# A smaller descriptor area for GpSimd's DMAs, and three more weight slabs kept in SBUF

## Chip, cores and metric

The kernel runs on one core of a Trainium2 chip. The metric is the device time of one execution in microseconds, from the first to the last instruction of the core. Three runs of the kernel before gave 2266.03 us (median), 2262.88 us (lowest) and 2273.69 us (highest). The profile is of one execution of 2273.2 us.

## The reference

The input `x` has 2048 rows of 1024 (bfloat16). It is layer-normed to `xn`, and the output is `x + A(xn) + B(xn)`.

- `B` is a dense block: `gelu(xn @ w1 + b1) @ w2 + b2`, with 3584 hidden columns.
- `A` is a recurrent attention layer. The 2048 rows are cut into 64 segments of 32 rows. Each segment puts 8 memory rows before its 32 rows, and runs 32-head attention (heads of 128) on the 40 rows:

```
for s in range(64):
    h = concat([mem, xn[32*s : 32*s+32]])          # 40 rows of 1024
    q, k, v = h @ Wq, h @ Wk, h @ Wv               # 1024 -> 4096 each
    p = softmax(mask(q @ k.T * scale))
    o = (p @ v) @ Wo                               # 4096 -> 1024
    mem, out[s] = o[:8], o[8:]
```

The new memory is part of the output of the segment before, so the 64 segments can't be computed together: every one needs all of Wq, Wk, Wv and Wo again. These are 4 x 1024 x 4096 bfloat16 numbers, 33.6 MB, which is more than SBUF holds.

## The kernel before

**Two stages.** The first stage (to about 360 us) is the dense block. It works on groups of 512 rows (`tg` from 0 to 3): transposed rows times w1 (L391), the gelu on ScalarE and VectorE (L384 to L407), times w2 (L438, and L471 in the last group). Its sum with `x` goes to HBM as the rows `R_n`, and the transposed normed rows go to `hr_d`, from which the second stage loads them segment by segment. The second stage is the loop over 64 segments (L567).

**Weights in units.** The four weights are cut into 64 units of [128, 2048] bfloat16: 4 KB in each partition, 512 KB in all. `pass_order` (L49) gives the order in which every segment uses them: eight units each of K, Q, V for the first 16 heads, eight each of K, Q, V for the other 16, then 16 units of O. A unit of K, Q or V is used by four matmuls of 512 columns that write four column groups of the array (L598), a unit of O by eight matmuls of 256 columns (L746).

43 of the units are resident: they are loaded once and stay in SBUF for all 64 segments. The other 21 are streamed: every segment loads them anew. The string `PLACED` (L65) says for each position of the order whether it is streamed. Streamed units are first copied in HBM to a dense layout (`copies`, L162, fetched at L425 in the first group of the dense block).

**The stream.** There are six stream buffers (`STREAM_BUFS`, L46). `start_stream` (L185) is called once for each streamed unit that has been used (`unit_done`, L542): the buffer of the unit that has just been used is given to the unit six further on in the stream, and SyncE issues its 512 KB DMA (L193). One streamed unit of each segment, `IN_PSUM` (L70, the fourth), doesn't come by DMA after the first segment: the first segment leaves it in two banks of PSUM (`keep_unit`, L518), and ScalarE and VectorE copy it from there to the buffer (L190, L191). So 20 DMAs of 512 KB are made per segment.

**Rows of several segments together.** Of each segment, 24 rows and the 8 memory rows go through the matmuls at once (`hT`); the other 8 rows of four segments are gathered and go through them once in four segments (`hL`). So one segment in four (`i4`, the segment's number modulo 4) has its K units used twice, another its Q units, another its V units, and another has the O units used with twice as many rows.

**Where SBUF goes.** The dense block's slabs (`PLACES`, L156: xn, w1, w2, gT) are 41 places of 4 KB per partition. The first six become the stream buffers, the other 35 take resident units as the dense block lets go of them (`fetch_resident`, L175, called at L458, L479 and L480). Eight more resident units are loaded in the first segment (`fetch_late`, L535). 16 KB of each partition, at address 0, are set aside by the library for the descriptors of the DMAs that GpSimd issues ("DynamicDMAScratchLoc").

**GpSimd's DMAs.** In the second stage GpSimd issues the small DMAs: the next segment's rows (`load_x_rows`, L199 to L202, called at L818 after the last V unit), the rows to be added to (L801, L807), the results (L852, L877 to L885), and in the first segments the rows `R_n` of the last group (L352). All of them are issued in the program's order on one queue. Some wait in the list `small` and are issued one or two at a time by `unit_done` after a streamed unit.

**The end of a segment.** After the 16 O units, ScalarE takes the sum from PSUM (L840), TensorE transposes the new memory rows (L222), VectorE puts them beside the rows that L201 loaded (L223), and the next segment's K pass starts.

Of the kernel before, what the change touches and what calls it, by code (L numbers as in the profile page):

```python
# [10 lines left out]
BF16 = mybir.dt.bfloat16  # L11
# [5 lines left out]
P = 128  # L17
S = 2048
# [23 lines left out]


NUNIT = 64
STREAMED = 21
STREAM_BUFS = 6  # L46


# [13 lines left out]


ORDER = pass_order()
PLACED = "S..S...S" "...S..S." "..S..S.." "S...S..S" "..S..S.S" "..S..S.." "S..S..S." ".S..S..S"  # L65
IS_STREAMED = {unit: PLACED[n] == "S" for n, unit in enumerate(ORDER)}
assert PLACED.count("S") == STREAMED
RESIDENT = [unit for unit in ORDER if not IS_STREAMED[unit]]
# [6 lines left out]
def kernel(  # L75
# [16 lines left out]
    nc = tc.nc  # L92
# [20 lines left out]
    outL_d = dram.tile([NGRP, 2 * SEG, DM], BF16, name="outL_d")  # L113
    outM_d = dram.tile([NGRP, P, 256], BF16, name="outM_d")

    slabs = ctx.enter_context(tc.tile_pool(name="slabs", bufs=1))
    consts = ctx.enter_context(tc.tile_pool(name="consts", bufs=1))
    hrp = ctx.enter_context(tc.tile_pool(name="hrp", bufs=1))
    ctx.enter_context(tc.manual_schedule())

    def slab(place):
        return slabs.tile([P, 2048], BF16, name="u", tag=place)


# [30 lines left out]

    PLACES = [f"xn{k}" for k in range(4)] + [f"w1_{k}" for k in range(16)]  # L156
    PLACES += [f"w2_{k}" for k in range(14)] + [f"gT{k}" for k in range(7)]
    STREAM_PLACES, RES_PLACES = PLACES[:STREAM_BUFS], PLACES[STREAM_BUFS:]
    res_tiles = {}


# [5 lines left out]
    def fetch(t, unit):  # L167
        w, i, u = unit
        if w == "O":
            h = 4 * i + 2 * u  # L170
            nc.sync.dma_start(out=t.rearrange("p (h d) -> p h d", d=DM), in_=Wo_v[:, h:h + 2, :])
        else:
            nc.sync.dma_start(out=t, in_=W_v[w][:, i, 2048 * u:2048 * u + 2048])

    def fetch_resident(n0, n1):  # L175
        for place, unit in list(zip(RES_PLACES, RESIDENT))[n0:n1]:
            res_tiles[unit] = slab(place)[:, :]
            fetch(res_tiles[unit], unit)
# [51 lines left out]
    with tc.tile_pool(name="ma", bufs=2) as ma, tc.tile_pool(name="mps", bufs=6, space=PSUM) as mps:  # L230
# [143 lines left out]
        for tg in range(4):  # L374
            last = tg == 3
            if last:

                load_x_rows(0)
                load_left_rows(0)
            gts = [slab(f"gT{i}")[:, :].rearrange("p (c t) -> p c t", c=4) for i in range(7)]  # L380

            def gelu_tail(fb, u, xb):
                sg = ma.tile([P, 512], BF16, name="g_sg")
                nc.scalar.activation(out=sg[:, :], in_=u[:, :], func=ACT.Sigmoid, scale=GELU_C)  # L384
                nc.vector.tensor_tensor(out=gts[fb // 4][:, fb % 4, :], in0=sg[:, :], in1=xb[:, :], op=ALU.mult)

            pend = None
            for fb in range(FC):
                ps = mps.tile([P, 512], F32, name="ps")
                for kt in range(KT):  # L390
                    nc.tensor.matmul(  # L391
                        ps[:, :].rearrange("p (s t) -> p s t", t=SEG),
                        lhsT=w1_sb[fb // 14 * 8 + kt][:, (fb % 14) * P:(fb % 14 + 1) * P],
                        rhs=xnT[kt // 4][:, :, kt % 4, :],
                        start=(kt == 0),
                        stop=(kt == KT - 1),
                    )
                xb = ma.tile([P, 512], BF16, name="g_xb", bufs=3)
                nc.scalar.activation(  # L399
                    out=xb[:, :], in_=ps[:, :], func=ACT.Identity, bias=b1col[:, fb:fb + 1], scale=1.0  # L400
                )
                u = ma.tile([P, 512], BF16, name="g_u")
                nc.vector.tensor_tensor(out=u[:, :], in0=xb[:, :], in1=xb[:, :], op=ALU.mult)
                nc.vector.tensor_scalar(
                    out=u[:, :], in0=u[:, :], scalar1=0.044715, scalar2=1.0, op0=ALU.mult, op1=ALU.add
                )
                nc.vector.tensor_tensor(out=u[:, :], in0=u[:, :], in1=xb[:, :], op=ALU.mult)  # L407
                if pend is not None:
                    gelu_tail(*pend)
                pend = (fb, u, xb)  # L410
            gelu_tail(*pend)

            if tg == 0:
                for nb in range(2):
                    cs = slice(nb * 512, nb * 512 + 512)
                    ps = mps.tile([P, 512], F32, name="ps")
                    nc.tensor.matmul(ps[:, :], lhsT=ones[0:1, :], rhs=b2row[0:1, cs], start=True, stop=True)
                    nc.scalar.copy(out=b2bc[:, cs], in_=ps[:, :])

            if not last:  # L420
                xnT = new_xnT(tg + 1)
                for t in range(4):
                    xtoks[4 * tg + 4 + t] = load_x(4 * tg + 4 + t)
                if tg == 0:
                    for unit, c in copies.items():  # L425
                        fetch(c, unit)
                for t in range(4):
                    ln_stats(4 * tg + 4 + t, xtoks[4 * tg + 4 + t])
                ln_rstd(4 * tg + 4, 4 * tg + 8)
                for t in range(4):  # L430
                    ttg = 4 * tg + t
                    xn = ln_apply(ttg + 4)
                    rsb = xtoks[ttg]
                    for nb in range(2):
                        cs = slice(nb * 512, (nb + 1) * 512)
                        ps = mps.tile([P, 512], F32, name="ps")
                        for fc in range(FC):
                            nc.tensor.matmul(  # L438
                                ps[:, :],
                                lhsT=gts[fc // 4][:, fc % 4, t * P:(t + 1) * P],  # L440
                                rhs=w2_sb[fc // 2][:, fc % 2, cs],
                                start=(fc == 0),
                                stop=(fc == FC - 1),
                            )
                        nc.vector.tensor_tensor(out=ps[:, :], in0=ps[:, :], in1=b2bc[:, cs], op=ALU.add)
                        nc.vector.tensor_tensor(out=rsb[:, cs], in0=ps[:, :], in1=rsb[:, cs], op=ALU.add)
                        if nb == 1:
                            turn_x(ttg + 4, xn, xnT)
                    keep_R(ttg, rsb)
                keep_xT(tg + 1, xnT)  # L450
                for t in range(4):
                    turn_R(4 * tg + t)
            else:


                for _ in range(STREAM_BUFS):
                    start_stream()
                fetch_resident(0, 16)  # L458
                put_mem(o_sb, nxt["hT"], mps.tile([P, KT, P], BF16, name="pT", bufs=2))
                pss = [mps.tile([P, 512], F32, name="ps") for _ in range(6)]  # L460
                pss += [mps.tile([P, 512], F32, name="pT", bufs=2) for _ in range(2)]
                for n in range(8):
                    cs = slice((n % 2) * 512, (n % 2 + 1) * 512)
                    nc.tensor.matmul(pss[n][:, :], lhsT=ones[0:1, :], rhs=b2row[0:1, cs], start=True, stop=False)
                    nc.tensor.matmul(
                        pss[n][:, :], lhsT=ident[:, :], rhs=xtoks[4 * tg + n // 2][:, cs], start=False, stop=False
                    )
                for fc in range(FC):
                    for t in range(4):
                        for nb in range(2):  # L470
                            nc.tensor.matmul(  # L471
                                pss[2 * t + nb][:, :],
                                lhsT=gts[fc // 4][:, fc % 4, t * P:(t + 1) * P],
                                rhs=w2_sb[fc // 2][:, fc % 2, nb * 512:nb * 512 + 512],
                                start=False,
                                stop=(fc == FC - 1),
                            )
                    if fc % 2:
                        fetch_resident(16 + fc // 2, 17 + fc // 2)  # L479
                fetch_resident(30, 37)  # L480
                for n in range(8):
                    cs = slice((n % 2) * 512, (n % 2 + 1) * 512)
                    cp = nc.scalar.copy if n % 2 else nc.vector.tensor_copy
                    cp(out=xtoks[4 * tg + n // 2][:, cs], in_=pss[n][:, :])
                for t in range(4):
                    keep_R(4 * tg + t, xtoks[4 * tg + t])
# [436 lines left out]
```

The softmax here doesn't subtract the row's maximum and nothing guards it: scores larger than these inputs give would overflow.

## Time and profile before

| what | before |
|---|---|
| median of three runs | 2266.03 us |
| span of the profile | 2273.2 us |
| TensorE busy | 2028.4 us (89%) |
| VectorE, ScalarE, GpSimd busy | 828.8, 660.5, 269.6 us |
| moved by DMA | 761.91 MB, 335 GB/s over the span |
| of it by the queue of SyncE | 736.71 MB |
| of it by GpSimd's DMAs | 16.87 MB in 16,000 packets |
| DMAs of 512 KB from the copies (L193) | 1281 |

The page's slices are 57 us each. "Busy" of TensorE includes matmuls whose ends are modelled, so that a busy TensorE isn't one at its peak, and a matmul that waits for less than its modelled end shows no idle time. A row of the chain of waits that reads "DMA u<-Wc_K" is the transfer of a streamed unit of K into a stream buffer. "issue" is time for which the profile shows no cause. A line such as L598 is line 598 of the kernel.

### The profile page before, as it was taken

What the parts mean: (1) busy time and instruction counts of PE and PEld (TensorE: products, weight loads), DVE (VectorE), ACT (ScalarE), POOL (GpSimd) and SP (SyncE); (2) the same over time, 40 slices, a digit from 0 to 9 for tenths busy, and PEclk for the clock granted to TensorE, in tenths of its full rate; (3) what the DMA queues carried; (4) which work ended last, traced back from release to release, by engine and by line L of the source; (5) the groups of instructions that cost most, each with busy time, mean ns of one, the idle gap of its engine ahead of it and who ended that gap; (6) DMA issues with size and microseconds to landing.
All of it is one profiled execution on the core that took longest, in us unless ns stands there. A gap on an engine that the chain in (4) does not pass through costs nothing.

```text
span 2273.2 us, 79002 instructions
## 1 busy us (share of the span) xinstructions
PE 2028.4 (89%) x34707; PEld 1047.3 (46%) x34707; DVE 828.8 (36%) x2264; ACT 660.5 (29%) x1540; POOL 269.6 (12%) x527
## 2 busy tenths in 40 slices
PE   7999999888898988898989898989898889888986
PEld 3444444344444444444544444444444444444443
DVE  6574844133333333333333333333323333333332
ACT  5251623122222222222222222222222222222222
POOL 0000000024111011111111111010111111111110
PEclk9999999999999999999999999999999999999999
DMA  9621116899999999999999999999999999999997
GB/s 323 205 71 33 51 51 230 296 395 391 388 402 371 384 373 388 362 382 386 386 379 401 377 397 374 395 372 374 376 372 372 376 383 400 378 379 378 401 382 276
DMA packets 256629, 761.91 MB, mean 335 GB/s; under 512 B 50923, under 2 KB 68283, under 8 KB 256284
## 3 DMA queue, kind: packets, MB, share of 16 engines
q1 hardware_dynamic: 234748, 736.71, 85.3%
q0 software_dynamic: 16000, 16.87, 2.2%
q8 instruction: 271, 4.44, 0.8%
q10 hardware_dynamic: 5536, 3.30, 0.5%
q14 instruction: 74, 0.61, 0.1%
HBM read 742.52 MB, written 33.10 MB: 341 GB/s over the span
## 4 chain that ended last, share of the span: by engine, by line
PE 66%; DMA 24%; DVE 3%; issue 3%; ACT 3%; POOL 0%; ACTq 0%; POOLq 0%; DVEq 0%; SPq 0%
PE acc L598 30%; PE acc L746 9%; PE ps L391 9%; DMA u<-Wc_O 7%; DMA u<-Wc_K 7%; PE ps L438 6%; DMA u<-Wc_V 5%; DMA u<-Wc_Q 4%; PE mixed L555 4%; PE acc L722 2%; PE ps L471 2%; PE mixed L685 1%; DVE d_oL L632 1%; PE mixed L681 1%; ACT d_oL L840 1%
## 5 line engine op out<-in xcount | busy, mean ns | idle before, releaser
L598 PE MATMUL acc<-u,hr 128*32 128x512 bf16 x12288 | 939.8, 391 | 74.6 <-DMA u<-Wc_Q 23.6
L598 PEld LDWEIGHTS <-hr 128*32 128x32 bf16 x12288 | 315.6, 97 | 379.0 <-issue 136.8
L598 PE MATMUL acc<-u,hrL 128*32 128x512 bf16 x3072 | 304.0, 384 | 3.5 <-issue 2.4
L626 ACT CAST d_oL<-acc 128x512 bf16<-128x512 f32 x192 | 112.4, 585 | 479.5 <-PE acc L598 435.4
L391 PE MATMUL ps<-u 128*128 128x512 bf16 x896 | 196.0, 382 | 2.6 <-ACT u L297 2.6
L642 DVE COPY kT<-mixed 128x512 bf16<-128x512 bf16 x128 | 54.4, 425 | 370.0 <-PE mixed L555 370.0
L746 PEld LDWEIGHTS <-b_oL 128*32 128x32 bf16 (+1 forms) x3552 | 136.1, 115 | 74.5 <-issue 64.0
L746 PE MATMUL acc<-W_O,b_oL 128*32 128x256 bf16 (+1 forms) x2220 | 130.0, 298 | 24.9 <-issue 24.9
L438 PE MATMUL ps<-u 128*128 128x512 bf16 x672 | 147.0, 379 | 0.0
L696 ACT ACTIVATE pr<-mixed 128x224 bf16<-128x224 f32 x128 | 45.7, 357 | 332.6 <-PE mixed L691 316.5
L391 PEld LDWEIGHTS <-u 128*128 128x128 bf16 x896 | 88.1, 98 | 109.2 <-issue 4.9
L746 PE MATMUL acc<-u,d_oL 128*32 128x256 bf16 (+1 forms) x2220 | 130.8, 294 | 4.9 <-DMA u<-Wc_O 2.5
L746 PEld LDWEIGHTS <-d_oL 128*32 128x32 bf16 (+1 forms) x3552 | 118.2, 112 | 33.1 <-issue 10.6
L652 DVE COPY b_oL<-mixed 128x512 bf16<-128x512 bf16 x128 | 54.4, 425 | 207.2 <-PE mixed L555 207.2
L746 PE MATMUL acc<-u,b_oL 128*32 128x256 bf16 (+1 forms) x1332 | 94.0, 300 | 26.1 <-DMA u<-Wc_O 15.2
L555 PEld LDWEIGHTS <-d_oL 128*128 128x128 bf16 x1020 | 59.4, 98 | 124.5 <-ACT d_oL L626 54.8
L598 PEld LDWEIGHTS <-hrL 128*32 128x32 bf16 x3072 | 86.0, 97 | 66.0 <-issue 9.0
L201 POOL DMA_DIRECT2D hr<-hr_d x63 | 34.6, 548 | 611.6 <-PE acc L598 351.3
L555 PE MATMUL mixed<-ident,d_oL 128*128 128x128 bf16 x896 | 89.3, 222 | 13.1 <-DVE d_oL L632 8.6
L438 PEld LDWEIGHTS <-u 128*128 128x128 bf16 x672 | 65.3, 98 | 77.4 <-DVE g_u L407 0.4
L734 ACT CAST d_oL<-acc 128x128 bf16<-128x128 f32 x128 | 50.9, 397 | 171.7 <-PE acc L728 171.7
L399 ACT ACTIVATE g_xb<-ps,b1col 128x512 bf16<-128x512 f32 x112 | 76.9, 686 | 61.0 <-PE ps L391 59.9
(126 smaller groups left out, 2408.4 us busy)
## 6 DMA issues: line engine op xcount, KB each, us to landing
u<-Wc_K SPq DMA_DIRECT2D x384, 512.0 KB
u<-Wc_O SPq DMA_DIRECT2D x384, 512.0 KB
u<-Wc_Q SPq DMA_DIRECT2D x257, 512.0 KB
u<-Wc_V SPq DMA_DIRECT2D x256, 512.0 KB
u<-in_B_w_dram SPq DMA_DIRECT2D x16, 448.0 KB
u<-in_B_w_dram SPq DMA_DIRECT2D x14, 512.0 KB
u<-in_A_Wv_dram SPq DMA_DIRECT2D x12, 512.0 KB
u<-in_A_Wq_dram SPq DMA_DIRECT2D x11, 512.0 KB
```

Source lines behind the costliest of these rows:

```text
L391: nc.tensor.matmul(ps[:, :].rearrange("p (s t) -> p s t", t=SEG), lhsT=w1_sb[fb // 14 * 8 + kt][:, (fb % 14) * P:(fb % 14 + 1) * P], rhs=x ...
L399: nc.scalar.activation(out=xb[:, :], in_=ps[:, :], func=ACT.Identity, bias=b1col[:, fb:fb + 1], scale=1.0)
L438: nc.tensor.matmul(ps[:, :], lhsT=gts[fc // 4][:, fc % 4, t * P:(t + 1) * P], rhs=w2_sb[fc // 2][:, fc % 2, cs], start=(fc == 0), stop=(fc ...
L471: nc.tensor.matmul(pss[2 * t + nb][:, :], lhsT=gts[fc // 4][:, fc % 4, t * P:(t + 1) * P], rhs=w2_sb[fc // 2][:, fc % 2, nb * 512:nb * 512 ...
L555: nc.tensor.transpose(dst[:, c, :], nat[:, c * P:(c + 1) * P], ident[:, :])
L598: nc.tensor.matmul(acc[32 * j:32 * j + 32, :], lhsT=lhs[:, i, :], rhs=t[:, 512 * j:512 * j + 512], start=(i == seq[0]), stop=(i == seq[-1] ...
L626: nc.scalar.copy(out=nat[:, :], in_=ps[:, :])
L642: nc.vector.tensor_copy(out=st["kT"][:, :, :], in_=by_head(tr))
L652: nc.vector.tensor_copy(out=st["qT"][:, :, 0:32], in_=by_head(tr))
L696: nc.scalar.activation(out=pr[:, :], in_=mixed[:, 0:224], func=ACT.Exp, scale=INV_SQRT_DH)
L734: cp(out=(o_both if left_o else o_main)[u][:, hs, 0:32], in_=oV[b][:, :, 0:32])
L746: nc.tensor.matmul(acc[r:r + n // 8, 0:n], lhsT=lhs[:, 4 * (i % 4) + 2 * u + k, :], rhs=t[:, 1024 * k + n * jq:1024 * k + n * jq + n], sta ...
```

## The change

The area for GpSimd's descriptors becomes 4 KB of each partition instead of 16 KB. The 12 KB that this frees hold three more resident units (`low0` to `low2`, tensors at fixed addresses right behind the smaller area). So 46 units are resident and 18 streamed, and one of the 18 stays in PSUM as before: 17 DMAs of 512 KB per segment instead of 20. The string `PLACED` is written anew, with the 18 streamed positions spread over the order: 2, 2, 2, 2, 2 and 3 in the passes K, Q, V, K, Q, V, and 2 and 3 in the two halves of O.

The three new places come first among the resident places. They are free from the start, so their units are fetched in the first group of the dense block, behind the copies, on SyncE's queue. The other calls of `fetch_resident` are shifted by three, so that each place of the dense block still takes its unit at the same point.

```diff
-STREAMED = 21
+STREAMED = 18
+LOW = 3
+SCRATCH = 4096
 STREAM_BUFS = 6
...
-PLACED = "S..S...S" "...S..S." "..S..S.." "S...S..S" "..S..S.S" "..S..S.." "S..S..S." ".S..S..S"
+PLACED = "S....S.." ".S....S." "..S..S.." ".S...S.." ".S..S..." "S..S...S" "..S...S." ".S...S.S"
...
+    place = nc.lookup_mloc("DynamicDMAScratchLoc")
+    assert place.addr == 0 and list(place.dims) == [P, SCRATCH + LOW * 4096]
+    nc.dynamic_dma_scratch_size = SCRATCH
+    place.dims = [P, SCRATCH]
+    nc.lookup_mls("DynamicDMAScratchLoc").tensor_shape = [P, SCRATCH]
+    low = {
+        f"low{k}": nc.alloc_sbuf_tensor_at(f"low{k}", [P, 2048], BF16, offset=SCRATCH + 4096 * k) for k in range(LOW)
+    }
...
     def slab(place):
+        if place in low:
+            return low[place]
         return slabs.tile([P, 2048], BF16, name="u", tag=place)
...
-    STREAM_PLACES, RES_PLACES = PLACES[:STREAM_BUFS], PLACES[STREAM_BUFS:]
+    STREAM_PLACES, RES_PLACES = PLACES[:STREAM_BUFS], list(low) + PLACES[STREAM_BUFS:]
...
                     for unit, c in copies.items():
                         fetch(c, unit)
+                    fetch_resident(0, LOW)
...
-                fetch_resident(0, 16)
+                fetch_resident(LOW, LOW + 16)
...
-                        fetch_resident(16 + fc // 2, 17 + fc // 2)
-                fetch_resident(30, 37)
+                        fetch_resident(LOW + 16 + fc // 2, LOW + 17 + fc // 2)
+                fetch_resident(LOW + 30, LOW + 37)
```

## The prediction

> **What bounds the kernel now.** I first cut the span into its stages with busy times by stretch, then asked the DMA view of the long stage what moves, and then the waits of TensorE in it. The ends of the stages are the two ends of VectorE's copies at L223, which close a segment: 64 of them, the first at 372 us, the second at 472.2, the last at 2231.0.
>
> ```profile
> 0.00:372.50 372.50, 354.49 (x1711) 163.70 (x1711) 235.98 (x593) 158.55 (x257) 11.54 (x43) 1.00 0.38 120
> 372.50:472.40 99.90, 87.75 (x947) 41.78 (x946) 16.84 (x41) 10.84 (x25) 0.70 (x1) 0.98 0.91 342
> 472.40:2231.00 1758.60, 1561.46 (x31640) 827.96 (x31640) 566.83 (x1608) 483.55 (x1240) 253.49 (x476) 0.98 1.00 383
> 2231.00:2273.20 42.20, 24.69 (x410) 13.86 (x410) 9.12 (x24) 7.58 (x18) 3.86 (x7) 0.88 0.59 230
> ```
>
> Columns: stretch, length, busy time of TensorE, its weight loads, VectorE, ScalarE and GpSimd, granted clock, DMA share, GB/s. The third row is what counts: 62 segments in 1758.6 us, 28.36 us each, with the 16 DMA engines busy all the time (1.00) at 383 GB/s. TensorE is idle for 1758.6 - 1561.5 = 197 us of it.
>
> ```profile
> DMA packets 199274, 673.43 MB, mean 383 GB/s; under 512 B 29294, under 2 KB 36258, under 8 KB 198966
> q1 hardware_dynamic: 178546, 650.13, 95.8%
> q0 software_dynamic: 15712, 16.60, 2.8%
> q8 instruction: 247, 4.05, 0.9%
> ```
>
> This is the same stretch by queue. The stream is 96% of it: 62 x 20 x 0.524 MB = 650 MB. Everything else is 23 MB. So the kernel is bound by its stream of weights.
>
> ```profile
> PE acc L746 <- issue: 38.9, 30, 2.5
> PE mixed L222 <- ACT d_oL L840: 28.7, 61, 0.5
> PE acc L598 <- DMA u<-Wc_Q: 20.4, 38, 1.6
> PE acc L598 <- DMA u<-Wc_K: 18.2, 45, 1.4
> PE acc L746 <- DMA u<-Wc_O: 17.4, 36, 1.0
> ...
> PE acc L598 <- DMA u<-Wc_V: 7.8, 18, 1.5
> ```
>
> TensorE's waits in it (us in total, times, longest). Those for streamed units sum to 20.4 + 18.2 + 17.4 + 7.8 = 63.8 us in 137 waits. That is smaller than a DMA-bound kernel suggests, because a wait hides behind the modelled end of the matmul before it:
>
> ```profile
> 1216.46 0.39 PE L598 MATMUL acc<-u,hr 128*32 128x512 bf16 x4
> 1216.68 0.39 PE L598 MATMUL acc<-u,hrL 128*32 128x512 bf16 x4
> 1216.89 0.39 PE L598 MATMUL acc<-u,hr 128*32 128x512 bf16 x4
> ```
>
> Start, length, and four matmuls each: they follow each other by 0.215 us and are drawn 0.39 long, so every visible wait cost 0.175 us more than shown, and shorter ones aren't seen. 137 x 0.175 = 24 us. The DMA waits are then 63.8 + 24 = 88 us, or 1.42 us per segment.
>
> **What the Trainium skill says.** "DMA: Bandwidth & Descriptors", Terms: a descriptor is 16 B, and those of GpSimd's DMAs are written to rings in SBUF; that area is what shrinks. No row shows a ring. "DMA: Bandwidth & Descriptors", Specifications: about 358 GB/s from HBM per core; the trace has 383, and I use that. "Runtime: NRT & Kernel Launch", Instruction fetch mechanics: instructions come in 16 KB blocks of 256, mostly hidden. The trace has the blocks (4.05 MB in 247 packets), but not always the hiding: the 38.9 us of L746 above have no cause but "issue", and L598 and L722 to L728 add 5.3. "TensorE: Matmul & The Clock Gate", What's actually happening: after an idle window of about 3.4 us the clock is halved. The trace agrees in kind: from 925.3 to 932.1 us the granted clock is 0.50, right after an issue wait of 2.44 us.
>
> **The change part by part.**
>
> *Three fewer transfers per segment.* 673.4 - 62 x 3 x 0.524 = 575.9 MB are left; at 383 GB/s that is 1504 us, 24.25 us per segment. The engines stop being the bound if TensorE needs longer than that, and it does: taking the DMA waits from the segment leaves 28.36 - 1.42 = 26.94 us. At that pace the engines would be 90% busy, with six buffers to run ahead by (six transfers of 1.37 us, 8 us of cover), so I expect DMA waits to be nearly gone, not only reduced. Even spacing is what allows that: the gaps of the new string are 2 to 5 positions within a segment.
>
> *What goes with these waits.* The mean granted clock is 0.98 in the stretch; the missing 0.02 x 1758.6 = 35 us are 0.57 us per segment lost at half clock. The halvings follow long waits, some for DMAs and some for instructions, so I take half of it away: 0.28. DMA waits below 0.175 us, which no view shows, I bound by 0 and 0.3 and take 0.15. Sum: 26.94 - 0.28 - 0.15 = 26.5 us. What stays is the instruction waits (38.9 + 5.3 = 44 us, 0.7 per segment), the end of a segment (L840, L222, L223), and the matmuls. The saving is 28.36 - 26.5 = 1.86 us, times 62: 115 us.
>
> *The first segment* (second row) is mostly bound by its loads: 34 MB in 99.9 us. It needs three fewer units, since those were fetched in the dense block: 3 x 0.524 MB at 383 GB/s is 4 us. The last segment with the output (42 us) has its DMA engines at 0.59, and its O pass is of the double kind: I count nothing.
>
> *The three early fetches, and 18 copies instead of 21.* They lie in the first group of the dense block, behind 354 of 372 us of busy TensorE and with the DMA engines at 0.38. Nothing.
>
> *PSUM unit, small DMAs.* The kept unit is the fourth streamed one still, and its buffer comes free at the same place of the order as before, the second O unit of the second half (number 57): ScalarE's 1.01 us and VectorE's 0.69 us stay where they are. The list `small` is emptied at 18 places instead of 21, for five entries or fewer in most segments. Nothing.
>
> *The 4 KB area.* GpSimd has 15,712 packets in 62 segments on 16 engines, 16 per engine and segment. If a packet is about one descriptor of 16 B, and 4 KB hold 256 of them for an engine, the area takes 16 segments' worth, while a DMA lands in about 5 us. The estimate rests on the skill's 16 B. I take no cost. The upper bound is a GpSimd that must wait for its DMA before to land. Queued behind it would be the next segment's rows, for which TensorE waits:
>
> ```profile
> DMA to landing us min/median/max: 4.7/5.4/6.6
> ```
>
> That is the landing time of L201's transfers; next is one of them in GpSimd's timeline, then VectorE's copy that needs its tile:
>
> ```profile
> 1230.90 0.53 POOL L201 DMA_DIRECT2D hr<-hr_d  x1 [0.96 <-PE acc L598]
> ```
>
> ```profile
> 1237.40 0.19 DVE L223 COPY hr<-mixed 128x64 bf16<-128x64 bf16 x1 [0.84 <-PE mixed L222]
> ```
>
> The rows are asked for at 1230.90 and needed at 1237.40: 6.5 us for a landing of 5.4 (6.6 at most). It fits, with 1.1 us to spare, and the O pass there is not much stretched by DMA waits, so a faster kernel keeps about that.
>
> Sum: 2266 - 115 - 4 = 2147 us.
>
> **The rivals.**
>
> *TensorE alone is left (chance 0.15).* All half clock and most instruction waits were the crowded DMA engines' doing. 28.36 - 1.42 - 0.57 - 0.7 - 0.15 = 25.5 us: 2266 - 62 x 2.84 - 4 = 2086. For it: the instruction blocks travel on the same engines. Against: the waits gather at L746, where instructions are used fastest (16 matmuls and weight loads per 0.217 us), which the change doesn't touch.
>
> *The stream still sets the pace (0.2).* Transfers start only when a buffer comes free, and with gaps the engines may not hold 383 GB/s. At the 342 GB/s of the first segment 9.29 MB take 27.2 us: 2266 - 62 x 1.16 - 4 = 2190. Against: these 342 come from a stretch with a share of 0.91.
>
> *The small area costs what the stream saves (0.07).* If GpSimd waited for one landing (5.4 us) ahead of the rows' load in each segment, 5.4 - 1.1 = 4.3 us would stand at every segment's end: 26.5 + 4.3 = 30.8, and 2266 + 62 x 2.44 - 4 = 2413 us, slower than before. If it met this only in the segments with O's double rows (one in four), 1.1 us on average, the time would be 2215. Against: the 16 segments of room. I give 0.04 to the slow end and 0.03 to between.
>
> **How the numbers follow.** The forecast (26.5 +- 0.4 us per segment) has 0.58. Its unknowns are the invisible waits (0 to 0.3) and the clock (0 to 0.57 of it): 25.9 to 27.0 us, or 2110 to 2178 us. The range reaches to both neighbours, to all of the second rival's 2190 and nearly to the first's 2086: 2090 to 2192. Faster 0.93; within 0.5% 0.03; slower 0.04.
>
> **What would show it.** The DMA share of the long stretch falls from 1.00 to about 0.9, its bytes to 576 MB; TensorE's waits for `u<-Wc_` fall from 63.8 to below 15 us; "issue" at L746 stays near 39 us; segments take 26.5 us; the stretch of the first segment falls by 4 us; GpSimd's busy time and the landing at L201 stay. A landing that ends the wait of L598 or L223, or GpSimd waiting in front of its DMAs, would show the small area's cost. The prediction is wrong if the DMA share stays at 1.00.

## The result, and the profile after

The changed kernel takes 2156.18 us (median; 2152.33 to 2160.28) against 2269.86 us of the kernel before in the same comparison. The ratio is 0.9486, with a 95% interval of 0.9451 to 0.9522: 114 us, or 5%, faster. 2147 us were forecast.

In the changed kernel the lines have moved: the matmuls of K, Q and V are L613 (before L598), those of O L761 (L746), the stream's DMAs L207 (L193), the rows' load L215 (L201), the copy that closes a segment L237 (L223).

Busy times by stretch, with the same columns as before (stretch, length, busy time of TensorE, weight loads, VectorE, ScalarE, GpSimd, granted clock, DMA share, GB/s). The stretches are again cut at the copy L237:

```profile
0.00:371.40 371.40, 353.61 (x1711) 163.47 (x1711) 236.05 (x593) 158.57 (x257) 11.54 (x43) 1.00 0.38 120
371.40:467.30 95.90, 87.44 (x947) 42.06 (x946) 16.81 (x41) 10.67 (x25) 0.70 (x1) 0.98 0.89 340
467.30:2118.50 1651.20, 1513.67 (x31640) 817.68 (x31640) 567.13 (x1608) 483.24 (x1240) 253.55 (x476) 0.99 0.96 349
2118.50:2152.20 33.70, 23.73 (x410) 13.55 (x410) 9.03 (x24) 7.65 (x18) 3.85 (x7) 0.95 0.64 241
```

The gain lies where it was looked for. The long stretch of 62 segments went from 1758.6 to 1651.2 us, 107.4 us shorter: 26.63 us per segment instead of 28.36. The first segment went from 99.9 to 95.9 us. The last stretch is 8.5 us shorter in these two profiles, which was not forecast; it isn't shown to be the change's doing, since the same stretch varies from 31 to 41 us among the profiles below (36.6 with the small area alone, 40.3 with the fewer transfers alone). VectorE, ScalarE and GpSimd did the same work in the same time.

The DMA view of the long stretch, and TensorE's waits in it (us in total, times, longest):

```profile
DMA packets 172287, 575.78 MB, mean 349 GB/s; under 512 B 26317, under 2 KB 33079, under 8 KB 171983
q1 hardware_dynamic: 151765, 552.62, 91.5%
q0 software_dynamic: 15712, 16.60, 3.1%
```

```profile
PE mixed L236 <- ACT d_oL L855: 29.3, 62, 0.5
PE acc L761 <- issue: 21.8, 22, 2.4
PE acc L737 <- DVE pr L725: 14.7, 43, 0.3
PE acc L613 <- DVE hr L237: 12.5, 44, 0.3
PE acc L613 <- DMA u<-Wc_Q: 8.9, 21, 0.9
...
PE acc L613 <- DMA u<-Wc_K: 2.9, 6, 1.2
...
PE acc L613 <- DMA u<-Wc_V: 0.9, 3, 0.5
...
PE acc L761 <- DMA u<-Wc_O: 0.3, 1, 0.3
```

The bytes are the 576 MB that were forecast. The waits for streamed units fell from 63.8 us in 137 waits to 13.0 us in 31. The issue wait at the O units fell too, from 38.9 to 21.8 us. TensorE's waits for results of VectorE and ScalarE rose: all of them together show 78 us in 205 waits before and 91 us in 249 after. The mean granted clock of the whole execution rose from 0.979 to 0.992. What didn't come is a visible rest for the DMA engines: their share is 0.96, though the rate is only 349 GB/s.

### The profile page after: what moved, and what is told of

The parts are those of the page before. It is cut to its first block, busy times and chain, and to the rows that moved or that the text cites. A ratio compares the mean times of both kernels' runs of the same rounds, so it can differ in the third digit from the quotient of the medians.

```text
span 2152.2 us, 78495 instructions
## 1 busy us (share of the span) xinstructions
PE 1978.5 (92%) x34707; PEld 1036.8 (48%) x34707; DVE 829.0 (39%) x2264; ACT 660.1 (31%) x1540; POOL 269.6 (13%) x527
## 4 chain that ended last, share of the span: by engine, by line
PE 73%; DMA 14%; ACT 5%; DVE 4%; issue 3%; POOL 0%; ACTq 0%; POOLq 0%; DVEq 0%; SPq 0%
PE acc L613 30%; PE acc L761 12%; PE ps L405 9%; PE ps L453 7%; DMA u<-Wc_Q 5%; PE mixed L570 4%; DMA outM_d<-res 3%; PE acc L737 3%; DMA res<-hr_d 2%; PE ps L486 2%; PE mixed L700 1%; PE acc L743 1%; ACT d_oL L750 1%; DMA u<-Wc_V 1%; PE mixed L719 1%
## 5 line engine op out<-in xcount | busy, mean ns | idle before, releaser
L613 PE MATMUL acc<-u,hr 128*32 128x512 bf16 x11520 | 873.6, 383 | 34.3 <-DVE hr L237 12.8
L613 PEld LDWEIGHTS <-hr 128*32 128x32 bf16 x12288 | 305.0, 96 | 318.2 <-issue 60.6
L613 PE MATMUL acc<-u,hrL 128*32 128x512 bf16 x2880 | 284.5, 380 | 0.0
L761 PEld LDWEIGHTS <-b_oL 128*32 128x32 bf16 (+1 forms) x3552 | 136.3, 114 | 31.4 <-issue 23.4
L761 PE MATMUL acc<-W_O,b_oL 128*32 128x256 bf16 (+1 forms) x2220 | 129.8, 295 | 9.3 <-issue 9.3
L761 PE MATMUL acc<-u,d_oL 128*32 128x256 bf16 (+1 forms) x2220 | 127.5, 293 | 4.0 <-issue 2.2
L761 PEld LDWEIGHTS <-d_oL 128*32 128x32 bf16 (+1 forms) x3552 | 118.7, 112 | 24.7 <-issue 8.4
L613 PEld LDWEIGHTS <-hrL 128*32 128x32 bf16 x3072 | 84.0, 97 | 64.2 <-issue 3.7
L215 POOL DMA_DIRECT2D hr<-hr_d x63 | 34.6, 549 | 577.0 <-PE acc L613 545.8
L761 PE MATMUL acc<-u,b_oL 128*32 128x256 bf16 (+1 forms) x1332 | 91.2, 295 | 10.7 <-issue 10.3
```

Of the source, the lines that this page charges most:

```text
L613: nc.tensor.matmul(acc[32 * j:32 * j + 32, :], lhsT=lhs[:, i, :], rhs=t[:, 512 * j:512 * j + 512], start=(i == seq[0]), stop=(i == seq[-1] ...
L761: nc.tensor.matmul(acc[r:r + n // 8, 0:n], lhsT=lhs[:, 4 * (i % 4) + 2 * u + k, :], rhs=t[:, 1024 * k + n * jq:1024 * k + n * jq + n], sta ...
```

## The experiments

Two theories were set against each other. The first is the prediction's: fewer transfers per segment, TensorE becoming the bound, and no cost in the small area. The other side had three parts: a cost of the small area, a stream that goes on setting the pace, and a gain that belongs to the placing. Each kernel below is given as its difference from the changed kernel, but for the one with the fewer transfers alone, which is given against the kernel before. A line of three dots stands for lines of the difference that are left out.

### The small area alone, and the fewer transfers alone

```diff
-STREAMED = 18
-LOW = 3
+STREAMED = 21
+LOW = 0
...
```

`PLACED` is that of the kernel before.

> The area for GpSimd's descriptors is 4 KB, the 12 KB behind it stay unused, and 21 units are streamed as placed before. Theory (the gain is three fewer transfers per segment, the small area costs nothing): the time of the kernel before, about 2268 us within 0.5%, GpSimd busy 270 us, no new wait in front of its DMAs. Rival (the small area has a cost that the saved transfers cover): slower than before by over 0.5%, 2280 us or more, if each segment pays 0.2 us or more.

Measured: 2261.96 us, a ratio of 0.9969 (0.9952 to 0.9987) to the kernel before. It isn't slower, but faster by 0.3% (8 us), with an interval that leaves out 1. The long stretch looks as before:

```profile
471.80:2228.70 1756.90, 1555.25 (x31640) 823.85 (x31640) 566.67 (x1610) 483.81 (x1240) 254.60 (x476) 0.98 1.00 384
```

The opposite half keeps the 16 KB, has no low places, and takes the transfers away. `STREAMED` and `PLACED` are those of the change; K1, K2 and K3 of the first half (K0 is the first unit) are not loaded, and K4 stands in for them:

```diff
+ALIASED = RESIDENT[:3]
+RESIDENT = RESIDENT[3:]
...
-            return res_tiles[unit]
+            return res_tiles[RESIDENT[0] if unit in ALIASED else unit]
```

> The area stays at 16 KB; 18 units are streamed, placed as in the change, and the three units that the change keeps in the freed space are not loaded at all: the resident unit K4 of the first half stands in for them, so their part of the product is computed with other weights. Theory (fewer transfers alone): the time of the change, 2156 us within 8 us. Rival (the small area costs something): faster than the change by more than 10 us, 2146 us or less.

Measured: 2159.49 us, ratio 0.951 (0.9474 to 0.9546), the time of the change. The two together show that all but about 0.3% of the 5% comes with the fewer transfers, and that 4 KB are enough for GpSimd's descriptors. No run shows what the 0.3% of the small area alone comes from.

### A still smaller area

```diff
-SCRATCH = 4096
+SCRATCH = 1024
...
```

The three units stay at their addresses.

> The change with an area of 1 KB instead of 4 KB, the three units where they are. Theory (GpSimd uses about 16 descriptors per engine and segment, so that 64 are four segments' worth): 2156 us within 8 us, GpSimd busy 270 us. Rival (the area is tight already): GpSimd waits for old transfers in front of its DMAs, the next rows come late, 2175 us or more.

Measured: 2145.28 us, ratio 0.9433 (0.9397 to 0.9468). It isn't slower than the change, whose interval it overlaps. GpSimd is busy for 254.06 us of the long stretch, with 253.55 in the change. The area isn't tight at 1 KB either. Nor do the 11 us show a gain: the changed kernel itself took 2149.32 us when it was run again (below).

### One unit and two units

```diff
-STREAMED = 18
-LOW = 3
-SCRATCH = 4096
+STREAMED = 20
+LOW = 1
+SCRATCH = 12288
...
+PLACED = "S...S..S" "...S..S." "..S..S.." ".S..S..." "S..S..S." ".S..S..S" "..S...S." ".S...S.S"
```

> Area of 12 KB, one more resident unit, 20 streamed, evenly placed. Theory (the bound passes between 20 and 18): 19 transfers and the rest need 27.0 us at 383 GB/s, a little more than TensorE's 26.6: about 27.2 us per segment, 2196 us, so the first unit alone brings two thirds of the gain. Rival (the time follows the bytes): a third of the gain, 2230 us.

Measured: 2229.74 us, ratio 0.982 (0.9776 to 0.9864).

```diff
+STREAMED = 19
+LOW = 2
+SCRATCH = 8192
...
+PLACED = "S...S..." "S...S..." "S...S..S" "...S...S" "..S...S." ".S..S..S" "..S...S." ".S...S.S"
```

> Area of 8 KB, two more resident units, 19 streamed, evenly placed. Theory (the bound passes from the DMA engines to TensorE between 20 and 18): 18 transfers and the rest need 25.6 us of a segment at 383 GB/s, less than the 26.6 us that TensorE takes in the change, so only some waits come back: about 26.8 us per segment, 2168 us. Rival (the time follows the bytes all the way): a third of the gain is lost, 2156 + 37 = 2193 us.

Measured: 2200.40 us, ratio 0.968 (0.9646 to 0.9715). Both times lie near the rival's, 2230 and 2193, and far from the theory's. 21, 20, 19 and 18 streamed units give 2270, 2230, 2200 and 2156 us: 40, 30 and 44 us for each. Down to 18 there is no point at which the bound passes to TensorE and the rest is free, and that part of the theory fell.

### Three units fewer than the change

```diff
-STREAMED = 18
+STREAMED = 15
...
+PLACED = "S....S.." "..S...S." "...S...S" "....S..." "S....S.." ".S....S." "...S...." ".S..S..S"
```

K1, K2 and K3 of the first half are not loaded, and K4 stands in for them.

> The change with 15 units streamed: three more units are not loaded, the resident unit K1 of the first half or another stands in for them, so their part of the product is computed with other weights. Theory (TensorE is the bound in the change): the waits for streamed units still there, 13 us shown in 31 waits and 0.175 us hidden in each, 18 us in all, vanish, and the first segment needs three transfers less, 4 us: about 2134 us. Rival (the stream still sets the pace): three transfers bring again what the first three did, about 2045 us.

Measured: 2099.83 us, ratio 0.923 (0.9196 to 0.9265). That is 56 us below the change, or 45 us below the change with 1 KB, which was run beside it: more than the 22 us of the theory, half or less of the 111 us of the rival. So three units now bring less than half of what the first three did. Now no wait for a streamed unit is worth a line, and the engines are idle for part of the time. By stretch, then TensorE's waits:

```profile
464.20:2066.90 1602.70, 1492.57 (x31640) 809.55 (x31640) 566.76 (x1609) 483.09 (x1240) 253.71 (x476) 1.00 0.87 299
```

```profile
PE mixed L238 <- ACT d_oL L857: 29.3, 62, 0.5
PE acc L739 <- DVE pr L727: 15.8, 46, 0.3
PE acc L615 <- DVE hr L239: 13.1, 46, 0.3
PE acc L763 <- issue: 12.9, 15, 1.6
```

The issue wait at the O units (L763 here) fell once more, from 21.8 to 12.9 us, and the clock is at 0.998. So these two weren't a floor of TensorE's own in the change; they go down with the stream. The time isn't far from the 2086 us of the prediction's first rival, in which TensorE alone is left.

### The placing

```diff
-PLACED = "S....S.." ".S....S." "..S..S.." ".S...S.." ".S..S..." "S..S...S" "..S...S." ".S...S.S"
+PLACED = "SSS....." ".....SSS" ".....SSS" ".....SSS" "........" ".....SSS" "........" ".S...S.S"
```

> The change with its 18 streamed units in five groups of three neighbours and the last three as in the change. Theory (six buffers, eight us of transfers, smooth that, since the engines have time to spare): some waits come back, 2156 to 2185 us. Rival (the even placing is a part of the gain of its own): the waits of the kernel before come back, 88 us or more: 2240 us.

Measured: 2341.16 us, ratio 1.0285 (1.024 to 1.033): slower than the kernel before, and slower than either theory allowed. The bytes are those of the change. In the first row below (the long stretch) the engines have a share of only 0.85; the next rows are pieces of one segment:

```profile
474.20:2310.90 1836.70, 1574.02 (x31640) 828.73 (x31640) 566.55 (x1609) 482.90 (x1240) 253.54 (x476) 0.97 0.85 313
1004.00:1007.00 3.00, 2.65 (x89) 2.02 (x89) 1.99 (x8) 1.38 (x5) 0.00 (x0) 1.00 1.00 401
1007.00:1009.00 2.00, 1.52 (x38) 1.08 (x38) 0.69 (x1) 0.94 (x2) 0.00 (x0) 1.00 0.35 113
...
1022.00:1028.00 6.00, 5.11 (x101) 2.52 (x103) 1.92 (x6) 1.99 (x6) 0.00 (x0) 1.00 1.02 407
1028.00:1031.00 3.00, 3.00 (x83) 1.52 (x79) 0.60 (x3) 0.26 (x1) 0.57 (x1) 1.00 0.33 120
```

```profile
PE acc L613 <- DMA u<-Wc_K: 89.6, 110, 2.2
PE acc L613 <- DMA u<-Wc_V: 42.6, 75, 2.0
...
PE acc L613 <- DMA u<-Wc_Q: 6.7, 11, 1.1
```

The engines run at over 400 GB/s for some us and fall to 113 or 120 when the stream has nothing to start. What they could have moved then is lost: TensorE waits for 139 us for units where it waited for 13. SyncE's timeline shows the issues in bursts, since buffers come free three at a time (start, length, transfers):

```profile
1001.62 1.40 SPq L207 DMA_DIRECT2D u<-Wc_K  x3
1007.98 0.80 SPq L207 DMA_DIRECT2D u<-Wc_Q  x2
```

From 1003.0, the end of the first burst, to 1008.0 nothing was issued: a transfer is issued only when TensorE is done with a unit, and it had no streamed unit to use. By 1007.0 the engines had moved what they had.

### Buffers instead of bytes

After these runs the theory was another one: what counts is how soon a buffer that comes free holds its next unit, against the time that six buffers give. The seventh buffer tests it at the same bytes:

```diff
-STREAM_BUFS = 6
+STREAM_BUFS = 7
-IN_PSUM = [unit for unit in ORDER if IS_STREAMED[unit]][3]
+IN_PSUM = [unit for unit in ORDER if IS_STREAMED[unit]][4]
+ALIASED = RESIDENT[:1]
+RESIDENT = RESIDENT[1:]
...
```

For this one the first resident unit, K1 of the first half, isn't loaded, and the second, K2, stands in. The unit kept in PSUM is the fifth streamed one instead of the fourth.

> The change with a seventh stream buffer in the place of one resident unit, which is not loaded: another resident unit stands in for it, so its part of the product is computed with other weights. 18 units are streamed, as placed in the change. Theory (what is left of the stream's waits comes from the time between a free buffer and its next landing, several us that six buffers just cover, not from the bytes): the 18 us of waits for units vanish, and a part of the instruction waits and the half clock with them, 2120 to 2140 us. Rival (the bytes alone set the pace): as the change, 2156 us.

Measured: 2130.28 us, ratio 0.9371 (0.9348 to 0.9394); the change itself, run beside it, took 2149.32 us (ratio 0.9468, 0.9428 to 0.9509). The 19 us are clear of both intervals. In the two profiles 17 us of the difference lie in the long stretch.

> The changed kernel itself, beside the three others of this call: 2156 us within 0.5%.

TensorE's waits with seven buffers:

```profile
PE acc L763 <- issue: 15.7, 17, 2.5
...
PE acc L615 <- DMA u<-Wc_Q: 1.2, 3, 0.6
PE acc L615 <- DMA u<-Wc_V: 1.0, 2, 0.6
```

The bytes are the same, and the waits for units are nearly gone: 2.2 us in five waits. So the waits for units left in the change were a matter of how far ahead six buffers can reach, not of bytes.

Two kernels that leave nothing out trade resident units for buffers. The first has 19 streamed units in the positions of the 19-unit kernel above, and seven buffers:

```diff
-STREAMED = 18
-STREAM_BUFS = 6
+STREAMED = 19
+STREAM_BUFS = 7
...
```

> A kernel with the small area that uses the three places for two more resident units and a seventh stream buffer: 19 streamed units in the positions of the 19-unit run before, nothing left out. Theory (landing time and number of buffers): most of the 39 us of waits of the 19-unit run with six buffers vanish, 2150 to 2165 us, as good as the change or better. Rival (bytes): as the 19-unit run with six buffers, 2200 us.

Measured: 2174.27 us, ratio 0.9559 (0.9525 to 0.9593). The seventh buffer takes 26 us off the 2200 of six, but not to the change's time. The waits for units went (29.5 to 6.5 us shown), the issue waits stayed (43.4 to 39.6 us). The second has 17 streamed units and five buffers:

```diff
+STREAMED = 17
+STREAM_BUFS = 5
...
+PLACED = "S....S.." "..S...S." "..S...S." "..S....S" "...S...S" "...S..S." "..S...S." ".S..S..S"
```

> The other way: a stream buffer is given to one more resident unit, five buffers and 17 streamed units, nothing left out. Theory (landing time and number of buffers): one transfer less but a loop of five buffers, the waits grow: 2180 us or more. Rival (bytes): a third of the gain again, about 2120 us.

Measured: 2154.61 us, ratio 0.9483 (0.9447 to 0.952). That is neither the 2180 of the one theory nor the 2120 of the other: one transfer fewer and one buffer fewer balance. No kernel that computes everything was found clearly faster than the change.

### The sum over all of them

For the long stretch of each kernel: the waits of TensorE for streamed units and for "issue", each as the waits view shows it plus 0.175 us per wait (the hidden part, as in the prediction), and the time lost at half clock, which is half of the time that the trace has the granted clock at 0.50 in the stretch. The 0.175 us were worked out for the matmuls at L598; those at L746 are drawn 0.27 long and follow each other by 0.11 in groups of four, so 0.16 us are hidden there, nearly the same.

| streamed units, buffers | stretch | units | issue | half clock | rest |
|---|---|---|---|---|---|
| 21, 6 (before) | 1758.6 | 89 | 52 | 41 | 1577 |
| 21, 6, area of 4 KB | 1756.9 | 87 | 55 | 32 | 1582 |
| 20, 6 | 1716.0 | 59 | 50 | 17 | 1590 |
| 19, 6 | 1689.6 | 38 | 50 | 15 | 1586 |
| 19, 7 | 1671.2 | 9 | 46 | 19 | 1597 |
| 18, 6 (change) | 1651.2 | 18 | 30 | 14 | 1589 |
| 18, 6 (change again) | 1643.4 | 20 | 24 | 10 | 1589 |
| 18, 6, area of 1 KB | 1638.0 | 19 | 25 | 9 | 1586 |
| 18, 6, area of 16 KB | 1643.5 | 24 | 23 | 9 | 1588 |
| 18, 7 | 1626.2 | 3 | 23 | 9 | 1592 |
| 17, 5 | 1648.5 | 29 | 26 | 9 | 1585 |
| 15, 6 | 1602.7 | 1 | 16 | 3 | 1582 |
| 18, 6, in groups | 1836.7 | 173 | 35 | 55 | 1574 |

All in us; 'before' counts two waits at the edge of the stretch that the prediction's list left out. Times from 1603 to 1837 us reduce to a rest of 1574 to 1597, which is 25.4 to 25.8 us per segment. Three losses make up the differences, down to the 20 us or so by which the rest itself varies, and all three were at work in the kernel before. The four kernels with 18 units, six buffers and even placing differ by 13 us among themselves, so smaller differences say nothing.

What the issue waits are can be read from the traces. The DMA view has a queue of kind "instruction", q8. In the long stretch of the change it has 247 packets for 63,280 matmuls and weight loads of TensorE, 256 to a packet. One issue wait at L761, and the queue in the 0.1 us from 1077.0, in which one of its packets started:

```profile
1079.27 0.27 PE L761 MATMUL acc<-u,b_oL 128*32 128x256 bf16 x1 [1.51 <-issue]
```

```profile
q8 instruction: 1, 0.02, 58.4%
```

By the packet records of the trace that packet ended at 1077.96, and the wait ended 1.31 us later. It is so every time: all 29 issue waits in the long stretch of the change, all 40 before, and all 388 in the thirteen traces end 1.2 to 1.6 us after a packet of q8 has ended, while these packets mostly start 6 to 7 us apart. So the issue waits are waits for blocks of instructions. The packets themselves take about 1 us in all these kernels, and so do those ahead of these waits (15 of the 388 took over 1.3 us), so what makes some blocks late comes mostly before their transfer starts. The half clock follows: all seven pieces of it in the long stretch of the change begin during an issue wait of 1.5 to 2.4 us or within 1.6 us of its end, this wait's too:

```profile
1080.30:1083.70 3.40, 3.40 (x36) 1.36 (x40) 0.52 (x2) 0.00 (x0) 2.05 (x4) 0.50 0.75 223
```

## Why the prediction was right, and where it was wrong

The time (2147 forecast, 2156 measured, 2149 when run again) and its main cause were right, and so was the sum for the long stretch: 115 us forecast, 107 measured and 115 when run again. But that it came so close is in part luck, since it came together from steps whose errors cancelled.

- *The waits for streamed units go.* Mostly right. 88 us were to vanish; 70 did, 18 are left. The step that failed is the cover: "six transfers of 1.37 us, 8 us of cover", with engines that are 90% busy, was to leave nearly no waits. Seven buffers at the same bytes leave 3 us, and grouping the same 18 units brings the waits to 173. Buffers have to come free in time for a transfer to start; that the engines have time to spare on average doesn't help. Nor was there much to spare: the stream's queue was without any packet for 1.5 us of the change's long stretch, against 1.4 us before, 48 us with 15 units and 115 us with the units in groups.
- *TensorE becomes the bound.* Only in part: the three units brought 40, 30 and 44 us, with no point between them from which more would be free; seven buffers take another 19 us off at the same bytes, and 15 units another 45 to 56 us. Stream and TensorE still hold each other up in the change.
- *The issue waits stay.* Wrong: 52 to 30 us with the hidden part (24 when run again), and 16 with 15 units streamed. The first rival had named the reason as its argument (the instruction blocks travel on the same engines), and the prediction held the place of these waits against it. The place is indeed the same, L761; their length goes with the stream. That they are waits for blocks of instructions is shown above; that a full stream is what makes a block late is argued, not shown, since no run changed the blocks alone.
- *Half of the clock loss goes.* Mis-sized: 35 us were seen and 17 of them taken; it was 41 us, and 27 went. It doesn't stand on its own, since it follows the long waits, of both kinds before and for instructions alone in the change. "TensorE: Matmul & The Clock Gate", What's actually happening, in the Trainium skill, has the halving after an idle window of about 3.4 us. The pieces at 0.50 in these traces last 3.41 us or twice that, which fits; but no wait in the long stretch reaches 3.4 us (2.5 is the longest before), so shorter waits were enough here. The prediction's example isn't quite "right after" its wait of 2.44 us either: the half clock began at 925.3, and the wait ended at 925.7.
- *Waits that can't be seen, 9 us.* Not found: the rest rose from 1577 to 1589 us rather than falling. The waits for VectorE and ScalarE, which are part of it, show 13 us more, so some of what was saved came back there.
- *Sum.* 88 + 0 + 17 + 9 = 114 us were forecast for the long stretch (115 before rounding) and 70 + 21 + 27 - 12 = 106 came (107 before rounding; it has to come out, since the rest is what is left over). The errors of the first and last step were made good by those of the issue waits and the clock. The range per segment doesn't follow from its own terms: the two unknowns give 26.1 to 26.9 us, not 25.9 to 27.0. The 26.6 us measured lie in both.
- *The first segment*, 4 us: 99.9 to 95.9 in these profiles, but 98.9 in the profiles of the change run again and of the 1 KB area. So it is 1 to 4 us, and the close hit is luck.
- *The small area costs nothing:* right, shown by the two halves and by 1 KB. The estimate behind it (16 descriptors per engine and segment) would give 1 KB four segments' worth, which is consistent with that; but what the traces count is 16 packets, and no view shows how many descriptors a packet takes. The slower rival falls with it.
- *The rows' landing.* The spare time was right in kind. The landing of L215 in the change, and what waited for it:

```profile
  DVE hr L237: 0.8, 1
...
DMA to landing us min/median/max: 4.2/5.3/6.7
```

One copy in 62 waited, for 0.8 us.

- *DMA share about 0.9.* Wrong: 0.96. The view counts the time that packets take, and these took longer: 0.915 x 16 x 1651.2 / 151765 = 0.159 us for a packet of SyncE's queue, where the kernel before has 0.958 x 16 x 1758.6 / 178546 = 0.151 us. Why they take longer isn't shown.
- *The rival "the stream still sets the pace"* named what the step of the cover left out: transfers start only when a buffer comes free, and seven buffers and the groups show that this counts. Its number fell. The rate did come down, to 349 GB/s, but 576 MB in the 26.5 us per segment of the forecast make 350 too, so the rate doesn't decide between them; and the 342 GB/s from which it computed 2190 us aren't a limit, as the 383 of the kernel before and the 401 and 407 in the pieces of the grouped kernel show.

Open is why the issue waits are 50 us with 20 and 19 streamed units and 23 to 30 us with 18. The seventh buffer barely moves them (46 with 19 units, 23 with 18), so the number of transfers seems to matter more than the waits for units; but nothing here tells the number of transfers apart from their timing.

## What to carry to other kernels

In a kernel that streams through a few buffers, bytes divided by bandwidth didn't give the time here: count how many buffers come free, when, and how long each needs to be filled, and space the streamed pieces evenly before anything else. A full DMA queue can also cost in places that don't look like DMA: here less was lost, with fewer transfers, in waits for instructions and in the halved clock that follows them, so relief past the point of balance still paid: 45 to 56 us for three transfers more. An area set aside by a library for descriptors may be far larger than a kernel needs, and a kernel with that area shrunk and nothing else changed tells whether it is.

## What the runs showed of the hardware that was not expected

- The DMA share falls less than the rate. From 383 to 349 to 299 GB/s it went 1.00, 0.96, 0.87, while a packet of SyncE's queue went from 0.151 to 0.159 to 0.167 us (0.814 x 16 x 1602.7 / 125124). A share near 1 isn't proof that the engines are the bound: with seven buffers it was 0.97 and the kernel was 19 us faster at the same bytes.
- All 388 issue waits of TensorE in the long stretches of thirteen traces end 1.2 to 1.6 us after the end of a packet that carries instructions, so a wait for which the profile shows no cause had one here.
- In the long stretch of the change the clock was halved for 3.41 us or twice that, each time beside an issue wait of 1.5 to 2.4 us; no wait of 3.4 us was needed.
- 18 transfers spread over a segment and the same 18 in groups of three differ by 185 us, or 8.6%.
- 1 KB of each partition is enough for the descriptors of GpSimd's 476 DMAs in the long stretch.
